# Gate rows made and stored during the first attention batch instead of after it, in a kernel of windowed attention and a four-expert mixture

## The chip, the cores and the metric

The kernel runs on one core of a Trainium2 chip. The metric is the device time of one execution, in microseconds (us). Three runs of the kernel before gave 365.98, 366.18 and 366.26 us; the median is 366.18 us. The profile is one further execution, recorded by the hardware profiler.

A core has a matrix engine (TensorE, here PE; its weight loads are shown apart as PEld), a vector engine (VectorE, DVE), an activation engine (ScalarE, ACT), GpSimd (POOL) and SyncE (SP). DMAs are issued from an engine's instruction stream, here from SP (q1 in the profile) and from POOL (q0), and all of them are carried out by the same 16 DMA engines. [...]

## The reference

Attention over 4 batches, 8 heads, 768 positions, 64 columns per head. A query sees the first 4 keys (sinks) and the last 128 keys. The result, 3072 tokens of 512 columns, goes through four experts, whose outputs are added with normalised weights:

```python
scores = scale * np.matmul(q, k.transpose(0, 1, 3, 2))
keep = is_sink | in_window
scores = np.where(keep, scores, -1000000000.0)
a = np.exp(scores - np.max(scores, axis=-1, keepdims=True))
a = a / (np.sum(a, axis=-1, keepdims=True) + 1e-09)
x = np.matmul(a, v)          # then heads side by side: (3072, 512)

p = domain_probs / (domain_probs.sum(-1, keepdims=True) + 1e-09)
for e in range(4):
    h = np.maximum(x @ w1[e], 0.0)         # w1[e]: 512 x 1024
    out += p[:, e:e + 1] * (h @ w2[e])     # w2[e]: 1024 x 512
```

The weight p of a token and an expert is called its gate.

## The kernel before

**Groups and units.** The tokens of a batch are three groups of 256: (b, 0), (b, 1), (b, 2). A unit is one group with one expert. The first layer of a unit makes H, the second layer adds it to the output.

**Two ways to apply the gate.** In groups (0, 0) and (0, 1) the second layer runs token by token (L1396), and the gate is applied to its result on DVE (L1406, L1408) as a scalar of each token. These scalars (`scale_t`) are made in `gates()`, with PE transposes of the raw gates (L907) and DVE operations (L909 to L912). From group (0, 2) on, the gate is applied to H itself, in the operation that empties a PSUM bank after the first layer (L1081, L1177). There the tokens lie along the free dimension, so each gate row of 256 tokens has to stand in all 128 partitions: a tile `gates` of 128 x 256 floats per unit.

**Where the gate tiles come from.** `gates_by_row()` works in `scratch`, where the raw gates of 24 blocks of 128 tokens lie since the start of the kernel: a sum over the experts, an addition, a reciprocal and a multiplication on DVE (L433 to L436), then two stores from SP to a DRAM tile `gate_rows` (L440). `load_gates()` asks for tiles in the order in which units will be opened (L456, SP), each a DMA that reads one row of 256 floats into 128 partitions. There are five buffers (NGATE): the first five tiles are asked for at once, a sixth when the unit that used the first is finished. `scratch` shares its buffer with the weight forms of expert 2 (`vf`), which come later.

**First and second layer.** A first layer is done plainly, in four tiles of eight matmuls of 256 columns (L1057, result `hps`), or with seven products in place of eight on sums of quarters (L1144, result `cps`), for which DVE makes forms of the weights (L376 to L382, L340 to L346) and differences of the tokens (L1113). The second layer of later groups is done likewise (L1318). Six PSUM banks are lent out in turn to all of these and to attention; two hold the second layer's sums.

**The order of the work.** The program is straight-line. Its order is found by a planner that runs while the program is built: it keeps a clock for each engine (`t["pe"]`, `t["dve"]`, ...), charges every operation an assumed time, and in a loop (from L1454) puts out the step that can start first, by priorities. `now` is PE's clock. Operations of ACT and DVE that follow a step are put on a list and put out by `flush` when the clock has come so far; some may go to either engine, whichever is free earlier. The planner does not know of the gate tiles' arrival: a unit is opened when its tokens, weights and banks are there. Each engine then works through its own instructions in the order written, waiting for semaphores.

**Order around the change.** Attention of batch 0 runs first, mixed with first and second layers of groups (0, 0) and (0, 1) once their tokens are ready. When its last step is out (`not att.more()`), a block of the loop runs once (`loaded`, L1460): gate rows, gate tiles, the list of loads of expert 3 and batch 1, and the list of DMA transposes of batch 1, which go on SP's queue (L245). From then on units of group (0, 2) may be opened (L1020). Weights and inputs are loaded by POOL, with a cast (L233, L298, L311, L321).

Of the kernel before, what the change touches and what calls it, by code (L numbers as in the profile page):

```python
# [16 lines left out]
def kernel(  # L17
# [63 lines left out]
    OPEN = 2.2  # L81
    SOON = 21000
    NEARLY = 2
    W2AT = 2
    ROWS1 = 1500
    ONACT = 1
# [30 lines left out]
    def dve(cols, *deps, rate=0.96, fixed=157):  # L117
        at = max([t["dve"], *deps])
        t["dve"] = at + fixed - 85 + cols / rate
        return at + fixed + 35 + cols / rate  # L120
# [232 lines left out]
    def spare_rows(e):  # L353

        spared[e] = [sb.tile([P, 2, H, D], BF16, name="qkn", tag="qkn", bufs=NQB) for _ in range(3)]
        spared_at[e] = qkn_free[2]
        del qkn_free[0:3]
# [28 lines left out]
    used, formed = set(), {}  # L386
    left = [NEARLY] * E

# [43 lines left out]
    def gates_by_row():  # L432
        nc.vector.reduce_sum(out=ds, in_=dp, axis=AX.X)  # L433
        nc.vector.tensor_scalar_add(out=ds, in0=ds, scalar1=1e-9)
        nc.vector.reciprocal(out=ds, in_=ds)
        nc.vector.tensor_mul(  # L436
            pn, dp.rearrange("n p e -> n e p"), ds[:, None, :].to_broadcast([NT, E, P]),
        )
        for i in range(2):
            nc.sync.dma_start(out=gate_rows[:, :, i, :], in_=pn[i:NT:2])  # L440
        dve(1800, 0.0)

    gate_sb = {}

    def load_gates():

        while len(gate_sb) < len(mix.order) and (
            len(gate_sb) < NGATE or mix.order[len(gate_sb) - NGATE] in mix.finished
        ):
            b, g, e = mix.order[len(gate_sb)]  # L450
            load_gate(b * NG + g, e)

    def load_gate(pair, e):

        x = mo.tile([P, 2, P], FP32, name="gates", tag="gates", bufs=NGATE)
        nc.sync.dma_start(  # L456
            out=x.rearrange("p t n -> p (t n)"), in_=gate_rows[pair, e].rearrange("t n -> (t n)").partition_broadcast(P),
        )
        gate_sb[pair, e] = x
        sp(takes=300)  # L460
# [362 lines left out]
    class Attention:  # L823


        def __init__(self, b):
            self.b = b
            self.flips = [("transposes", b, g, hp) for g in range(NG) for hp in range(NHP)] if not b else []
            self.todo, self.scored, self.valued = [], [], []
            for g in range(NG):  # L830
                if g == (1 if b == 0 else 0):
                    self.todo.append(("keys", b, 0, 0))
                self.todo += [("scores", b, hp, g) for hp in range(NHP)]
                if g and (b < ONE or g == 1):
                    self.todo.insert(2 - NHP if b == 0 else -NHP, ("sinks", b, g, 1 if b < ONE else 2))
            self.total = len(self.todo) + len(self.flips) + (1 if b else 2) * NG * NHP
            self.steps = 0
# [80 lines left out]
    QF = NFB // 2  # L918
    PAIRS = [(b, g) for b in range(B) for g in range(NG) if (b, g) >= (0, NEARLY)]
    CHAIN = ("P1", "P2", "P6", "P5", "P7", "P3", "P4")  # L920
# [3 lines left out]
    class Mixture:  # L924


        def __init__(self):
            self.early = {g: list(range(E)) for g in range(NEARLY)}
            self.open = []
# [159 lines left out]
        def tokens(self):  # L1089

            pairs = [x for x in [(0, g) for g in range(NEARLY)] + PAIRS if any(self.is_fast(*x, e) for e in FAST)]
            n = len(self.T)
# [128 lines left out]
        def chore(self):  # L1221
# [25 lines left out]
            if any(x[:2] < (b, g) and x[2] == "P5" for x in self.products) or any(x[:2] < (b, g) for x in self.last):  # L1247
                return False
            if (b, g) == PAIRS[0] and (len(self.stored) < 2 * NEARLY or self.stored[-1] > t["pe"] + 500):
                return False  # L1250
# [177 lines left out]
    mix = Mixture()  # L1428
    att = Attention(0)
    work = [sum(NFB * NDB * G * (1 if (b, g) < START[e] else 7 / 8) + NFB * NDB * G * (1 if (b, g) < PAIRS[0] else 7 / 8) for g in range(NG) for e in range(E)) for b in range(B)]  # L1430
    ahead, upto, loaded, wide = 0, 0.0, 0, 0
    loads, turns = [(load_nat, 0, tb) for tb in (4, 5)] + [(load_v, 0, (4, 5))], []
    for e in (1, 2):
        loads += [(load_w1, e), (load_w2, e)]
# [7 lines left out]
    def load_ready(x):  # L1442
        if x[0] is load_nat:
            return qkn_free[0]
        if x[0] is load_v and x[1]:
            return max(values_at.get((x[1] - 1, min(NG - 1, (tb + 1) // 2)), 1e12) for tb in x[2])
        return 0.0

    def free_ring(x):
        if ahead < 1 or turns and x[1] <= turns[0][0]:  # L1450
            return True
        return t["hw"] < t["pe"] and not (turns and (turns[0][0], 0) in turned_at)

    while mix.more() or att.more():  # L1454
        now = t["pe"]

        if not att.more() and ahead == B - 1 and not wide:
            wide = 1
            mix.widened()
        if not att.more() and not loaded:  # L1460
            loaded = 1
            gates_by_row()
            load_gates()
            turns += [(1, tb) for tb in range(NQB)]
            loads.append((load_w1, 3))
            for tb in range(NQB):
                if tb == W2AT:
                    loads.append((load_w2, 3))
                loads.append((load_nat, 1, tb))
                if tb % 2:  # L1470
                    loads += [(load_v, 1, (tb - 1,)), (load_v, 1, (tb,))]
        x = next((x for x in loads if load_ready(x) < now + 1500), None)
        if x and t["pool"] < now + 1500 and free_ring(x):
            loads.remove(x)
            x[0](*x[1:])
        if turns and (ahead < 2 or not mix.second) and landed.get(("qk", *turns[0]), 1e12) < now and (turns[0][0] <= ahead or turns[0][0] == ahead + 1 and not att.todo):
            x = turns.pop(0)
            turn_nat(*x)
            b = x[0]
            if b in (1, B - 1) and x[1] == NQB - 1:  # L1480
                spare_rows("w2" if b == 1 else "w1")
            if 0 < b < B - 1 and x[1] == NQB - 1:
                nc.gpsimd.tensor_copy(out=held, in_=qkT[b][:, 1, NHP - 1, S - 2:S])
                pool(2, turned_at[x])
                nat_loads(b + 1, range(NQB))
                turns += [(b + 1, tb) for tb in range(NQB)]
        flush(now)
        mix.tokens()
        mix.chore()
        if ahead or now > SOON:  # L1490
            next_form()
        if ahead + 1 < B and not att.more() and (ahead == 0 or (ahead + 1, 0) in turned_at) and (ahead == 0 or mix.done >= sum(work[:ahead]) * LEAD[ahead - 1]):
            ahead += 1
            att = Attention(ahead)
            upto = mix.done
        share = (sum(work[:ahead]) - upto) * SHARE_OF[max(ahead - 1, 0)]
        due = ahead == 0 or att.steps * share <= (mix.done - upto) * att.total
        opts = []
        if att.more():
            opts = [(max(r, now), (DUE if due else 3) - 0.1 * (step == "two"), "att", step) for r, step in att.options()]  # L1500
        s2, p = mix.second_ready(), mix.product_ready()
        behind = max(t["dve"] - now, 0.0) + 500 * sum(x[2] == "dve" and x[0] < now + 300 for x in pend)
        opts.append((max(p, now), HIGH_PRODUCT if behind > BEHIND or mix.live >= FULL else LOW_PRODUCT, "product", None))
        opts += [(max(f, now), p, "first", x) for f, p, x in mix.firsts()]
        opts.append((max(s2, now), 1 if mix.since >= 1 else LOW_SECOND, "second", None))
        soonest = min(o[0] for o in opts)
        if soonest > now + 40 and flush(soonest, True):
            continue
        if soonest < 20000 and soonest > now + 220:
            idle_products(acc[1], 1, G)  # L1510
            continue
        if soonest > 1e11:
            if mix.stored and mix.stored[-1] > now:
                t["pe"] += 200
            elif loads:
                x = loads.pop(0)
                x[0](*x[1:])
            else:
                turn_nat(*turns.pop(0))
            continue  # L1520
        r, _, kind, step = min(opts, key=lambda o: (o[0] > now + 40, o[0] if o[0] > now + 40 else 0, o[1]))
        assert r < 1e11
        if kind == "att":
            att.emit(step)
        elif kind == "first":
            mix.emit_first(step, r)
        elif kind == "product":
            mix.emit_product()
        else:
            mix.emit_second()  # L1530
# [36 lines left out]
```

## Time and profile before

| | |
|---|---|
| median of three runs | 366.18 us (365.98 to 366.26) |
| the profiled execution | 366.61 us |
| its span, first to last instruction | 364.9 us |
| mean granted clock of PE | 0.995 |
| busy: PE, PEld, DVE, ACT, POOL | 352.8, 302.6, 303.9, 162.7, 71.5 us |
| DMA moved | 37.79 MB, mean 104 GB/s |

The span is cut by the profile's views into waits (who stood still until whom), a chain (followed back from the last instruction to what released each step), and stretches with the busy time of each engine. The granted clock is the share of full speed at which PE was let run. Idle time of an engine that does not bound a stretch costs nothing.

### The profile page before, as it was taken

The page shows a single profiled execution, that of the slowest core. Times are in us where ns is not written, and L with a number is a line of the kernel's source. Part 1 is how long each engine was busy: PE and PEld are TensorE (multiplying, and loading weights), DVE is VectorE, ACT ScalarE, POOL GpSimd, SP SyncE. Part 2 cuts the span into 40 slices and gives each one's busy share as a digit, 9 for nine tenths or more (in the row PEclk, how much of TensorE's full clock was granted, in tenths as well). Part 3 has the DMA queues.
Part 4 walks back from the last instruction along what each step waited for, and adds up shares of the span by engine and source line. Part 5 has one row for each costly group of instructions (what it writes and reads, how often), then busy time and mean ns, then how long its engine had stood idle before and what let it go on. Part 6 is the DMA issues. An engine that isn't in the chain of part 4 may idle for free.

```text
span 364.9 us, 10705 instructions
## 1 busy us (share of the span) xinstructions
PE 352.8 (97%) x4476; PEld 302.6 (83%) x4484; DVE 303.9 (83%) x690; ACT 162.7 (45%) x415; POOL 71.5 (20%) x92
## 2 busy tenths in 40 slices
PE   7899995999999999999999999999999999999995
PEld 3585763866689898898998999899899999999984
DVE  6875965968799989889769999989879889899840
ACT  5864610626786264556454344444435333313110
POOL 8936113440434406001052000000000000000000
PEclk9999998999999999999999999999999999999999
DMA  9999999999999999318199923011211031110011
GB/s 166 168 181 195 210 210 200 181 135 153 143 117 162 180 162 122 61 43 104 31 137 167 136 72 59 25 55 41 59 42 48 25 81 59 31 43 18 3 59 58
DMA packets 117869, 37.79 MB, mean 104 GB/s; under 512 B 100676, under 2 KB 113316, under 8 KB 117820
## 3 DMA queue, kind: packets, MB, share of 16 engines
q0 software_dynamic: 77520, 17.31, 53.5%
q1 hardware_dynamic: 39244, 19.28, 26.8%
q8 instruction: 35, 0.57, 0.6%
q10 hardware_dynamic: 1056, 0.52, 0.5%
q14 instruction: 14, 0.11, 0.1%
HBM read 40.98 MB, written 6.34 MB: 130 GB/s over the span
## 4 chain that ended last, share of the span: by engine, by line
PE 87%; DMA 5%; DVE 4%; POOL 2%; ACT 1%; issue 1%; SPq 0%; DVEq 0%; ACTq 0%
PE acc L1318 34%; PE cps L1144 32%; PE hps L1057 9%; PE acc L1396 5%; PE sps L683 3%; PE od L749 2%; DMA w<-in_moe_w_dram 2%; DMA gates<-gate_rows 2%; DMA gate_rows<-scratch 1%; POOL qkn L233 1%; PE od L742 1%; POOL vx L298 1%; DVE aT L717 0%; DVE onat L779 0%; ACT aT L708 0%
## 5 line engine op out<-in xcount | busy, mean ns | idle before, releaser
L1144 PEld LDWEIGHTS <-w 128*128 128x128 bf16 x1184 | 72.6, 98 | 3.0 <-issue 1.6
L1318 PEld LDWEIGHTS <-H 128*128 128x128 bf16 x700 | 65.0, 98 | 8.0 <-issue 1.5
L1177 DVE SCALAR_TENSOR_TENSOR H<-cps,gates 128x512 bf16<-128x512 f32 x90 | 60.7, 684 | 0.1
L708 ACT ACTIVATE aT<-sps 128x512 bf16<-128x512 f32 (+1 forms) x96 | 46.9, 571 | 24.7 <-PE sps L683 24.7
L1318 PE MATMUL acc<-w,H 128*128 128x256 bf16 x420 | 55.4, 273 | 0.0
L1057 PE MATMUL hps<-xT,w 128*128 128x256 bf16 x352 | 44.9, 278 | 3.9 <-DVE H L1081 3.8
L1144 PEld LDWEIGHTS <-vf 128*128 128x128 bf16 x744 | 45.6, 98 | 1.2 <-issue 0.5
L1144 PE MATMUL cps<-T,w 128*128 128x128 bf16 x592 | 45.0, 219 | 0.6 <-DVE cps L1197 0.6
L1144 PE MATMUL cps<-xT,w 128*128 128x128 bf16 x592 | 43.7, 219 | 0.0
L788 ACT ACTIVATE onat<-od,R 128x64 bf16<-128x64 f32 x144 | 33.2, 323 | 23.0 <-DVE R L776 22.9
L1057 PEld LDWEIGHTS <-w 128*128 128x128 bf16 x352 | 34.0, 100 | 10.7 <-issue 4.9
L1190 ACT COPY cps<-cps 128x512 f32<-128x512 f32 x37 | 21.4, 578 | 47.6 <-PE cps L1144 27.5
L1144 PE MATMUL cps<-T,vf 128*128 128x128 bf16 x496 | 36.4, 219 | 0.0
L1368 ACT COPY osb<-acc 128x256 f32<-128x256 f32 x36 | 13.6, 377 | 50.5 <-PE acc L1318 50.5
L298 POOL DMA_DIRECT2D vx<-in_v_dram x24 | 21.4, 896 | 62.6 <-PE od L749 52.7
L1318 PEld LDWEIGHTS <-S 128*128 128x128 bf16 x320 | 30.4, 98 | 3.4 <-issue 0.2
L1197 DVE TENSOR_TENSOR cps<-H,cps 128x512 f32<-128x512 f32 x32 | 22.2, 693 | 9.7 <-PE cps L1144 8.4
L1396 PE MATMUL acc<-w,H 128*128 128x512 bf16 x120 | 29.3, 379 | 0.6 <-issue 0.3
L1318 PE MATMUL acc<-wf,H 128*128 128x256 bf16 x208 | 29.3, 273 | 0.0
L702 DVE TENSOR_TENSOR aT<-aT,mask 128x1024 bf16<-128x1024 bf16 (+1 forms) x36 | 22.8, 643 | 3.5 <-ACT aT L708 3.2
L1212 DVE TENSOR_TENSOR H<-H,cps 128x512 f32<-128x512 f32 x32 | 21.9, 684 | 2.7 <-PE cps L1144 2.6
L1396 PEld LDWEIGHTS <-H 128*128 128x128 bf16 x128 | 12.1, 98 | 12.1 <-issue 0.2
(128 smaller groups left out, 548.1 us busy)
## 6 DMA issues: line engine op xcount, KB each, us to landing
w<-in_moe_w_dram POOLq DMA_DIRECT2D x7, 1024.0 KB, 18.5
out_dram<-osb SPq DMA_DIRECT2D x21, 256.0 KB
gates<-gate_rows SPq DMA_DIRECT2D x40, 128.0 KB
vx<-in_v_dram POOLq DMA_DIRECT2D x24, 128.0 KB, 6.3
qkn<-in_q_dram POOLq DMA_DIRECT2D x22, 128.0 KB, 8.6
qkn<-in_k_dram POOLq DMA_DIRECT2D x22, 128.0 KB, 9.6
w<-in_moe_w_dram POOLq DMA_DIRECT2D x2, 512.0 KB, 9.0
kraw<-in_k_dram ACTq DMA_DIRECT2D x2, 256.0 KB
```

The lines of the kernel that those rows point to most:

```text
L298: nc.gpsimd.dma_start(out=vx[tb][:, :, 0:D], in_=v[b, :, tb * P:(tb + 1) * P, :].rearrange("h p d -> p h d"),)
L702: nc.vector.tensor_mul(a, a, m[:, None, :].to_broadcast([P, 2, w]))
L708: nc.scalar.activation(out=a[:, ph], in_=sps[ph][:, 0:w], func=AF.Exp, scale=scale)
L788: nc.scalar.mul(o[:, qi, hp, ph * D:(ph + 1) * D], od[:, qi, ph, 0:D], R[:, qi, ph])
L1057: nc.tensor.matmul(h[:, i].rearrange("p (q n) -> p q n", q=2), lhsT=w1_sb[e][:, db, fb * P:(fb + 1) * P], rhs=xT[b, g][:, :, db], start=(i ...
L1144: nc.tensor.matmul(y[:, f], lhsT=A[:, d, f * P:(f + 1) * P], rhs=T[:, d], start=(m in ("P1", "P5") and f == 0 and d == 0), stop=(d == 1), ...
L1177: nc.vector.scalar_tensor_tensor(out=dst, in0=src, scalar=0.0, in1=gate, op0=ALU.max, op1=ALU.mult)
L1190: nc.scalar.copy(out=tiles["Y"], in_=y)
L1197: nc.vector.tensor_add(tiles["V"], c5, tiles["X"])
L1212: nc.vector.tensor_add(c5, c5, y)
L1318: nc.tensor.matmul(x, lhsT=self.operand(b, g, e, m)[:, f], rhs=forms[e][m][:, f], start=(k == 0 and f == 0 and m in (("P1", "P5", "P2") if ...
L1396: nc.tensor.matmul(op, lhsT=H[:, fb // QF, fb % QF, s], rhs=w2_sb[e][:, fb, :], start=(fb == 0), stop=(fb == NFB - 1),)
```

## The change

The making and storing of the gate rows and the request for the first gate tiles leave the block that runs after batch 0's attention. They get a condition of their own: the first time that PE's planned clock is past 24000 (ns) at the head of the loop. The block keeps its loads and transposes. The planner's charge for the four DVE operations goes from 1800 to 2800 columns.

```diff
+    ROWED = 24000
...
         for i in range(2):
             nc.sync.dma_start(out=gate_rows[:, :, i, :], in_=pn[i:NT:2])
-        dve(1800, 0.0)
+        dve(2800, 0.0)
...
+        if not rowed and now > ROWED:
+            rowed = 1
+            gates_by_row()
+            load_gates()
         if not att.more() and not loaded:
             loaded = 1
-            gates_by_row()
-            load_gates()
             turns += [(1, tb) for tb in range(NQB)]
             loads.append((load_w1, 3))
```

The four DVE operations, the two stores and the loads of the tiles are the same instructions as before; their places in the streams of DVE and SP differ, and whatever the planner orders otherwise because its clocks differ.

More of the change, by code (lines that the diff above doesn't have):

```diff
@@ L1430 @@
     work = [sum(NFB * NDB * G * (1 if (b, g) < START[e] else 7 / 8) + NFB * NDB * G * (1 if (b, g) < PAIRS[0] else 7 / 8) for g in range(NG) for e in range(E)) for b in range(B)]
-    ahead, upto, loaded, wide = 0, 0.0, 0, 0
+    ahead, upto, loaded, wide, rowed = 0, 0.0, 0, 0, 0
     loads, turns = [(load_nat, 0, tb) for tb in (4, 5)] + [(load_v, 0, (4, 5))], []
```

## The prediction

> **What bounds the kernel now.** I read the page's first and fourth parts, then the waits of the matmul engine (PE), the chain of waits, and the stretches between 46 and 75 us.
>
> ```profile
> span 364.9 us, 10705 instructions
> PE 352.8 (97%) x4476; PEld 302.6 (83%) x4484; DVE 303.9 (83%) x690; ACT 162.7 (45%) x415; POOL 71.5 (20%) x92
> ```
>
> PE is the bound: 352.8 of 364.9 us. What can be won is the 12 us in which it stands still, and time at a lower clock. The waits of PE (total, times, longest):
>
> ```profile
> PE hps L1057 <- DVE H L1081: 3.8, 1, 3.8
> PE cps L1144 <- DVE cps L1197: 0.6, 1, 0.6
> ```
>
> The 3.8 us are one wait: the first-layer tiles of group (0,2) for expert 0 find no free PSUM bank, because VectorE (DVE) has not multiplied the earlier tile by its gate. The chain of waits, in order of time (start, us, what), says why DVE is late:
>
> ```profile
> 43.89 0.95 DVE scratch L435
> 44.86 1.07 DVE scratch L436
> 46.92 5.42 DMA gate_rows<-scratch
> 52.39 6.15 DMA gates<-gate_rows
> 59.38 3.52 PE hps L1057 x16
> ```
>
> The gate rows are made at 43 to 46 us, stored, and read back as tiles: two DMAs in series, 11.6 us, landing at 58.54. The stretches around it (columns: span, PE, PEld, DVE, ACT, POOL busy, PE clock, DMA share, GB/s):
>
> ```profile
> 46.00:55.60 9.60, 9.55 (x64) 6.18 (x64) 5.84 (x12) 1.79 (x3) 1.75 (x2) 1.00 1.24 207
> 55.60:59.40 3.80, 0.04 (x2) 0.01 (x1) 0.76 (x2) 0.00 (x0) 0.17 (x1) 0.97 1.85 209
> 59.40:62.80 3.40, 3.40 (x18) 2.29 (x18) 3.37 (x6) 0.00 (x0) 1.75 (x3) 0.53 1.95 198
> 66.00:67.00 1.00, 0.41 (x9) 0.29 (x7) 1.00 (x3) 0.42 (x1) 1.00 (x2) 1.00 1.29 210
> 75.00:361.00 286.00, 285.72 (x3797) 256.02 (x3798) 248.26 (x549) 125.70 (x342) 35.65 (x42) 1.00 0.64 82
> ```
>
> PE is empty from 55.6 to 59.4, then runs 3.40 us at clock 0.53, and has one more hole at 66 while DVE works off its backlog. From 75 to 361 us it misses only 0.28 us. So all that this change can give lies between 55 and 67 us.
>
> **The change part by part.** *Where the rows go.* The new condition is looked at once per planned step, in the planner's own clock. That clock charges a first-layer tile 8 x 256 / 2.4 + 8 x 2.5 = 873 ns, the step of the tiles in the row at 23.05 below (40 matmuls, five tiles; the last four are group (0,1)). Following its arithmetic, 24000 is first passed ahead of the third tile of that group, which is at 23.05 + 3 x 0.87 = 25.7 us in the trace. At that point the last DVE work put out is the fourth token difference. DVE in order of time (start, us, operation, idle before):
>
> ```profile
> 24.19 0.28 DVE L1113 TENSOR_TENSOR T<-xT,T 128x256 bf16<-128x256 bf16 x1
> 24.39 0.68 DVE L376 TENSOR_TENSOR vf<-w 128x1024 bf16<-128x1024 bf16 x1
> 28.20 0.26 DVE L909 TENSOR_REDUCE rs<-acc 128x24 f32<-128x96 f32 x1 [2.40 <-PE acc L907]
> 31.77 0.75 DVE L1406 TENSOR_SCALAR osb<-acc,scale_t 128x512 f32<-128x512 f32 x1 [0.97 <-PE acc L1396]
> 34.38 0.75 DVE L1406 TENSOR_SCALAR osb<-acc,scale_t 128x512 f32<-128x512 f32 x1 [1.54 <-PE acc L1396]
> 42.94 0.67 DVE L433 TENSOR_REDUCE scratch<-scratch 24x128 f32<-24x512 f32 x1
> 58.64 0.69 DVE L1081 SCALAR_TENSOR_TENSOR H<-hps,gates 128x512 bf16<-128x512 f32 x1 [6.66 <-DMA gates<-gate_rows]
> ```
>
> *The four DVE operations.* They run from 42.94 to 44.86 + 1.07 = 45.93, so 2.99 us, of which nothing is saved. Moved, they run from 24.47 to 27.46. The weight forms of L376 and L378 step back behind them (by the planner's clock behind the scale operations of L909 too). Idle stretches of 2.40, 0.97 and 1.54 us, 4.9 in sum, take the 3 us before anything of PE waits; were they not there, PE would lose at most the 2.99 us. I take 0. The other end: DVE, busy 5.84 us of the time from 46 us to the start of its long idle (58.64 - 6.66 = 51.98), is 2.99 us freer there; PE, busy 9.55 of 9.60 us, can't turn that into time.
>
> *Larger planner cost (1800 to 2800).* No instruction; it moves planned times only, see the plan below.
>
> *SP's queue.* SyncE, in order of time:
>
> ```profile
> 2.42 5.69 SPq L473 DMA_DIRECT2D vsf<-in_v_dram  x8
> 45.96 1.73 SPq L440 DMA_DIRECT2D gate_rows<-scratch  x2
> 52.39 12.93 SPq L456 DMA_DIRECT2D gates<-gate_rows  x6
> 65.51 5.93 SPq L245 DMA_TRANSPOSE qkT<-qkn  x2
> ```
>
> SP is empty from 8.1 to 46 us, so the two stores and five loads, and the wait of the loads for the stores, hold up nothing. Row stores: issued at 27.5, landed 52.39 - 45.96 = 6.4 us later, 33.9. First tile 6.15 us on, 40.0; all five some 9 us after the first issue, 43. The first is wanted when DVE gets to it, at 51.98. So 9 to 12 us to spare and the 6.66 us idle of DVE goes. The sixth load waits for a gate buffer, and batch 1's transposes are behind it; both come earlier by the same shift, and their first reader is PE's row at 83.59 below, far off. POOL's queue gets nothing and is passed by nothing.
>
> *What goes.* PE's wait, 3.76 us. The half clock behind it: 3.40 x (1 - 0.53) = 1.60 us. The hole at 66, where DVE at 100% was catching up: 0.59 us. Sum 5.95 us.
>
> *What it collides with.* Five tiles of 128 x 256 floats are 0.66 MB, the rows 0.05. They now move while weights are being read, and two of those are wanted soon. PE's rows, POOL's issues, and the time to landing of the two loads (w1 and w2 of expert 1, last column):
>
> ```profile
> 23.05 4.53 PE L1057 MATMUL hps<-xT,w 128*128 128x256 bf16 x40
> 38.62 1.04 PE L1057 MATMUL hps<-xT,w 128*128 128x256 bf16 x8
> 44.19 1.89 PE L1396 MATMUL acc<-w,H 128*128 128x512 bf16 x7
> 83.59 0.50 PE L683 MATMUL sps<-qkT 64*128 64x256 bf16 x8
> 21.90 0.75 POOL L311 DMA_DIRECT2D w<-in_moe_w_dram  x1 [1.35 <-DMA w<-in_moe_w_dram]
> 27.66 0.88 POOL L321 DMA_DIRECT2D w<-in_moe_w_dram  x1 [5.00 <-DMA w<-in_moe_w_dram]
> w<-in_moe_w_dram POOLq DMA_DIRECT2D x1, 1024.0 KB, 15.1
> w<-in_moe_w_dram POOLq DMA_DIRECT2D x1, 1024.0 KB, 14.4
> ```
>
> w1 lands at 37.0 and is read at 38.62: 1.6 us to spare. w2 lands at 42.06 and is read at 44.19: 2.1 us. What the gate tiles took from the weights is in the DMA queues (packets, MB, share of 16 engines), first from 52.4 to 56.2 us, then from 56.2 to 61.2:
>
> ```profile
> q0 software_dynamic: 1432, 0.72, 140.5%
> q1 hardware_dynamic: 8, 0.01, 0.8%
> ...
> q0 software_dynamic: 3265, 0.44, 131.3%
> q1 hardware_dynamic: 712, 0.65, 48.6%
> ```
>
> The weights fell from 0.72 / 3.8 = 0.19 to 0.44 / 5.0 = 0.09 MB per us for five us: 0.5 MB pushed back, at 207 GB/s 2.5 us. And the tiles' packets began only 3.8 us after the first issue. Carried over: they move from about 37.7 to 42.7, w1 (37.0) is gone by then, w2 comes at most 2.5 us late, 44.6 against 44.19. Cost 0.4 us. One end is 0: the tiles come after w2's own packets. The other is a start without the lag of 3.8 us, for stores and tiles both: the stores land near 30, the tiles run from 30 to 35, w1 comes at 37.0 + 2.5 = 39.5 against 38.62, PE waits 0.9 us there and no more at w2. I take the lag, since the q1 row shows it.
>
> [...]
>
> *The plan behind it.* From 42 us on the planner sees DVE earlier by its old charge (about 1.9 us), so operations that either engine may take, and steps that come free a little sooner, can change place. Matmul work is the same either way. The trace before has no row for another order. It can win at most the 0.28 us that PE still misses after 75; it can lose a wait like those of the trace, 0.6 or 3.8 us. I take 0.6, the nearest of its kind (PE on DVE behind a backlog).
>
> *Sum.* -5.95 + 0.4 + 0.6 = -4.95 us. The profiled execution took 366.61 us in all (span 364.9 and 1.7 around it), 0.43 above the median of 366.18. So 361.7 for that execution, 361.2 against the median.
>
> **The rivals.**
>
> *Tiles without the lag.* The 0.9 us above in place of 0.4: 361.7.
>
> *Weights late.* The tiles drag on, at the rate of the row from 56.2 to 61.2 but for ten us in place of five: 10 x (0.19 - 0.09) / 0.207 = 4.9 us, so w2 at 47.0 and a wait of 2.8 us. 366.18 - 5.95 + 2.8 + 0.6 = 363.6, with 363 to 364.5 around it. For: only 1.6 and 2.1 us to spare. Against: the bytes are few, 0.71 MB is 3.4 us at 207 GB/s in all.
>
> *DVE takes its place: slower.* DVE is full when batch 1 begins its own experts:
>
> ```profile
> 60.00:70.00 10.00, 9.96 (x17) 0.87 1.71 193
> 100.00:110.00 10.00, 9.96 (x23) 1.00 1.36 119
> 110.00:120.00 10.00, 10.00 (x26) 1.00 1.61 163
> ```
>
> (Columns: span, DVE busy, PE clock, DMA share, GB/s.) PE arrives there about 5 us sooner. If DVE did not, or if the new order put another 2 to 3 us of its work in these 20 us, PE would wait for it one for one, and a wait near 4 us also costs 1.6 us of clock, as at 59. It decides when the waits pass 5.95 us, say one of 4.0 with its 1.6 of clock and one of 2.0: 7.6, so 366.2 + 7.6 - 5.95 = 367.9 us. For: no slack in these rows. Against: DVE gains the 6.66 us of idle at 52 that PE's lead comes from, so both arrive earlier together.
>
> *The change does not do it: same.* If the rows are put behind something late, or SP held, the tiles still land near 51 to 58 and the wait remains: 366.2. SP's empty queue and the free DVE from 24 to 35 speak against it.
>
> *Small loss by the new order.* A second wait of 2 to 3 us somewhere after 75: 363 to 364.5.
>
> **How the numbers follow.** Forecast (gain 3.2 to 6.3): 0.65, its own range 359.9 to 363.0; 0.12 of that are tiles without the lag. Weights late, 363 to 364.5: 0.13. Small loss by order, the same span: 0.08. Same: 0.04. DVE takes its place: 0.10. A difference under 0.2% (0.7 us) is about what a measurement of this kernel can't tell from none. Faster 0.86, same 0.04, slower 0.10. Lower bound: 366.18 - 5.95 - 0.28 with no collision, 359.95; a little under, 359.7. Upper: beyond 365.2 lie the last two cases, 0.14.
>
> **What would show it.** Right: the four operations near 24.5 to 27.5 on DVE, the stores right behind on SP, the gate tiles landed before 45, no wait of PE on L1081, clock 1.00 from 55 to 65, DVE without the 6.66 us idle. The collision: a wait of PE on the weight DMA near 44 of 0.4 us (or near 39 of 0.9). Wrong: such a wait over 2 us, DMA landings of w1 and w2 over 3 us later, a new idle of PE over 1 us between 75 and 361, or the gates' DMA still ending DVE's wait.

## The result and the profile after

The changed kernel takes 361.65 us (median of six runs, 361.21 to 363.26) against 366.08 us of the kernel before beside it. The ratio is 0.9884, with a 95% interval of 0.9867 to 0.9900: 1.2% faster. Two later comparisons, each on a chip of its own, gave 0.9888 (0.9858 to 0.9917) and 0.9869 (0.9851 to 0.9886).

The profiled execution of the changed kernel took 363.26 us, the slowest of its six; the second profile of it, below, shows in which waits. One line was added above most of the code, so line numbers are mostly one higher than before. The first lines of the page:

```profile
span 361.5 us, 10704 instructions
PE 351.5 (97%) x4476; PEld 302.4 (84%) x4484; DVE 303.8 (84%) x691; ACT 162.4 (45%) x414; POOL 71.7 (20%) x92
```

The span is 3.4 us shorter and PE is busy 1.3 us less: it did the same 4476 matmuls, but none at half clock (1.00 in every stretch up to 357.6 us). The stretches that had carried the loss (span, PE, PEld, DVE, ACT, POOL busy, PE clock, DMA share, GB/s):

```profile
46.00:55.60 9.60, 9.28 (x61) 6.13 (x63) 5.98 (x10) 1.79 (x3) 1.75 (x2) 1.00 1.19 209
55.60:59.40 3.80, 3.80 (x31) 2.66 (x29) 3.64 (x7) 0.00 (x0) 0.87 (x1) 1.00 1.77 180
59.40:62.80 3.40, 3.40 (x62) 3.28 (x60) 3.40 (x6) 2.04 (x4) 1.34 (x2) 1.00 2.26 163
66.00:67.00 1.00, 1.00 (x22) 1.00 (x20) 1.00 (x4) 1.00 (x3) 0.65 (x1) 1.00 1.26 205
75.00:357.60 282.60, 281.52 (x3762) 253.25 (x3762) 244.09 (x542) 124.14 (x339) 35.40 (x42) 1.00 0.67 84
```

PE is full from 55.6 to 62.8 and at 66, at clock 1.00. But from 75 us to the end of the matmuls it now misses 1.08 us where it missed 0.28. The waits of PE that are new, in the same view as before (total, times, longest):

```profile
PE acc L1397 <- DMA w<-in_moe_w_dram: 1.3, 1, 1.3
PE hps L1058 <- DMA w<-in_moe_w_dram: 0.9, 1, 0.9
PE sinks L645 <- DVE qkn L345: 0.8, 1, 0.8
```

The wait for the gate is gone. In its place stand a wait for the second-layer weights of expert 1, one at the very start for the first expert's weights, and one at the sink scores of batch 1. Where PE stands at these three waits, and at its first tile with seven products in place of eight (59.23), in the changed kernel:

```profile
19.73 0.50 PE L1058 MATMUL hps<-xT,w 128*128 128x256 bf16 x3 [0.90 <-DMA w<-in_moe_w_dram]
...
46.21 1.89 PE L1397 MATMUL acc<-w,H 128*128 128x512 bf16 x7 [1.32 <-DMA w<-in_moe_w_dram]
...
59.23 0.61 PE L1145 MATMUL cps<-xT,w 128*128 128x128 bf16 x8
...
89.45 0.29 PE L645 MATMUL sinks<-qkT,ksd 128*32 128x256 bf16 x4 [0.85 <-DVE qkn L345]
```

and the kernel before at the first of them, at that tile, and at the sink scores:

```profile
19.11 1.05 PE L1057 MATMUL hps<-xT,w 128*128 128x256 bf16 x8 [0.15 <-DMA w<-in_moe_w_dram]
...
62.74 0.28 PE L1144 MATMUL cps<-xT,w 128*128 128x128 bf16 x2
...
92.80 0.29 PE L644 MATMUL sinks<-qkT,ksd 128*32 128x256 bf16 x4
```

So this execution was 0.62 us behind at 19 us, before anything of the change, and 2.02 us behind at the second layer (46.21 against 44.19). At the first tile with seven products it was 3.51 us ahead (59.23 against 62.74). Between these two places it gained 2.02 + 3.51 = 5.53 us, close to the wait and the half clock of the prediction (3.76 + 1.60 = 5.36). The last stretch of matmuls starts 3.36 us sooner (338.53 against 341.89).

The rows and tiles went where the prediction put them. DVE and SP in order of time:

```profile
24.94 0.67 DVE L434 TENSOR_REDUCE scratch<-scratch 24x128 f32<-24x512 f32 x1
...
26.87 1.07 DVE L437 TENSOR_TENSOR scratch<-scratch 24x512 f32<-24x512 f32 x1
28.75 0.26 DVE L910 TENSOR_REDUCE rs<-acc 128x24 f32<-128x96 f32 x1 [0.82 <-PE acc L908]
```

```profile
27.96 1.72 SPq L441 DMA_DIRECT2D gate_rows<-scratch  x2
34.66 26.13 SPq L457 DMA_DIRECT2D gates<-gate_rows  x6
...
77.77 5.61 SPq L246 DMA_TRANSPOSE qkT<-qkn  x2
83.48 0.55 SPq L1415 DMA_DIRECT2D out_dram<-osb  x1
```

The second pair of transposes in the kernel before:

```profile
77.68 4.89 SPq L245 DMA_TRANSPOSE qkT<-qkn  x2
```

The four operations take 3.00 us and end at 27.94; the stores are issued at 27.96; the first tile load 6.7 us later.

Instruction by instruction, the streams of PE, POOL and SP are in the same order in both kernels. DVE's differs by the rows' place and a few neighbours, and one copy went from ACT to DVE. The planner ordered hardly anything else otherwise.

### The profile page after: what moved, and what is told of

Same layout as the page of the kernel before. It is cut to its first block, busy times and chain, and to the rows that moved or that the text cites. A ratio compares the mean times of both kernels' runs of the same rounds, so it can differ in the third digit from the quotient of the medians.

```text
span 361.5 us, 10704 instructions
## 1 busy us (share of the span) xinstructions
PE 351.5 (97%) x4476; PEld 302.4 (84%) x4484; DVE 303.8 (84%) x691; ACT 162.4 (45%) x414; POOL 71.7 (20%) x92
## 4 chain that ended last, share of the span: by engine, by line
PE 86%; DMA 11%; DVE 1%; issue 1%; ACT 1%; POOL 0%; ACTq 0%; POOLq 0%; DVEq 0%
PE acc L1319 34%; PE cps L1145 32%; DMA w<-in_moe_w_dram 9%; PE hps L1058 7%; PE acc L1397 6%; PE sps L684 3%; PE od L750 2%; DMA kraw<-in_k_dram 2%; PE od L743 1%; PE sinks L645 0%; ACT aT L709 0%; POOL w L312 0%; DVE qkn L345 0%; DVE qkn L343 0%; ACT qkn L270 0%
## 5 line engine op out<-in xcount | busy, mean ns | idle before, releaser
L1058 PE MATMUL hps<-xT,w 128*128 128x256 bf16 x352 | 43.3, 273 | 0.9 <-DMA w<-in_moe_w_dram 0.9
L1198 DVE TENSOR_TENSOR cps<-H,cps 128x512 f32<-128x512 f32 x32 | 22.1, 691 | 9.8 <-PE cps L1145 8.4
## 6 DMA issues: line engine op xcount, KB each, us to landing
w<-in_moe_w_dram POOLq DMA_DIRECT2D x7, 1024.0 KB, 18.3
```

The costliest lines, as they stand in the source:

```text
L1058: nc.tensor.matmul(h[:, i].rearrange("p (q n) -> p q n", q=2), lhsT=w1_sb[e][:, db, fb * P:(fb + 1) * P], rhs=xT[b, g][:, :, db], start=(i ...
L1198: nc.vector.tensor_add(tiles["V"], c5, tiles["X"])
```

## The experiments

Two theories at the start. The first: the gain is the removed wait with its half clock, and what is missing from it is DMA time, the tiles' packets pushing back loads that PE then waits for. The rival: part of gain and loss comes from the other order on DVE and ACT.

### Early rows in the old order

```diff
-        dve(2800, 0.0)                 # in gates_by_row
...
             loaded = 1
+            dve(1800, 0.0)
```

> Rows and tiles early as in the changed kernel, but the planner's charge stays where and what it was (1800, when attention is over), so that ACT's stream and the rest of DVE's are those of the kernel before. If the gain is the gate wait alone, this one gains as much as the changed kernel: 361.7 us within 0.6, with the wait for the second-layer weights near 46 us of about 1.3. If part of the gain or loss comes from the other order on DVE and ACT, it lies more than 0.7 us off.

In the traces the order of every stream is that of the kernel before, apart from the four operations. 361.72 us, ratio 0.9866 (0.9835 to 0.9896): all of the gain, without the new order. Its profiled execution took 361.55 us, and after 20 us PE waits for one thing of note:

```profile
PE sinks L644 <- DMA qkT<-qkn: 1.0, 1, 1.0
```

The weights' wait that I expected there is absent. The sink scores' wait stands, and here the view names the DMA, batch 1's transposes, and not DVE. It is the same wait in the changed kernel: there the last of these transposes landed at 89.31 us by the trace, and the sink scores started at 89.45.

### Late rows in the new order

```diff
         if not rowed and now > ROWED:
             rowed = 1
-            gates_by_row()             # its own charge is taken out
-            load_gates()
+            dve(2800, 0.0)
...
             loaded = 1
+            gates_by_row()
+            load_gates()
```

> The streams of ACT and the rest of DVE as in the changed kernel (charge of 2800 at 24000), but the four operations, stores and tile loads back after attention. If the order alone does nothing: 366.1 us within 0.7, wait of PE on L1081's successor of about 3.8 and the half clock behind it. If the order is worth something of its own: below 365.

In the traces the order is that of the changed kernel, apart from the four operations. 365.94 us, ratio 0.9982 (0.9962 to 1.0002). The order alone is worth nothing that can be told from zero; the wait is back, 2.98 us and then 0.67, and so is the half clock:

```profile
58.74 1.19 PE L1057 MATMUL hps<-xT,w 128*128 128x256 bf16 x8 [2.98 <-DVE H L1081]
60.59 1.86 PE L1057 MATMUL hps<-xT,w 128*128 128x256 bf16 x8 [0.67 <-DVE H L1081]
```

```profile
60.00:61.00 1.00, 0.41 (x3) 0.27 (x3) 1.00 (x2) 0.00 (x0) 0.69 (x1) 0.50 1.77 221
61.00:62.00 1.00, 1.00 (x6) 0.71 (x5) 0.97 (x3) 0.00 (x0) 0.55 (x1) 0.50 2.43 155
```

The rival falls: place of the rows, not order, makes the difference.

### Early rows, tiles held back

```diff
-            load_gates()               # behind gates_by_row() in the early block
...
             loaded = 1
+            load_gates()
...
         x = mo.tile([P, 2, P], FP32, name="gates", tag="gates", bufs=NGATE)
+        if not gate_sb:
+            nc.vector.memset(x[:, 0, 0:2], 0.0)
```

> Rows made and stored early, but the first gate tile's load has to follow a small write of DVE to that tile, put out when attention is over (near 42 us); the other four are behind it on SP. If the wait for the second-layer weights near 46 us (1.3 us) comes from the tiles' packets, it goes, the weights land near 42.5 in place of 46.2, and the time falls by 0.6 to 1.3 us below the changed kernel: 360.4 to 361.0. If that wait has another cause, it stays and the time is 361.7. If the tiles now come too late for L1081, DVE waits for them near 53 and the time rises above 362.

361.59 us, ratio 0.9851 (0.9829 to 0.9873). No wait for the second-layer weights is left, and none for the tiles; the sink scores' wait of 0.8 us stays. In time it is not the 360.4 to 361.0 expected but level with the early rows in the old order on the same chip (361.72), which had no such wait either. So the tiles cost a wait in some executions, and a gain in time from holding them is not shown. How long the weights take from issue to landing (last column), in the kernel before, with the tiles held back, and in the changed kernel:

```profile
w<-in_moe_w_dram POOLq DMA_DIRECT2D x1, 1024.0 KB, 14.4
```

```profile
w<-in_moe_w_dram POOLq DMA_DIRECT2D x1, 1024.0 KB, 14.8
```

```profile
w<-in_moe_w_dram POOLq DMA_DIRECT2D x1, 1024.0 KB, 18.3
```

In two more profiles of the changed kernel it was 17.3 and 17.0 us, with the early rows in the old order 17.3. The tiles hold this load up by 2.2 to 3.9 us (17.0 against 14.8, 18.3 against 14.4). Whether PE feels it depends also on when POOL issued it: at 26.24 us with the early rows in the old order (landed 43.54, read at 44.17, no wait), at 27.91 us in the changed kernel's first profile (landed 46.21).

### Twice the tiles

```diff
+        if len(gate_sb) < NGATE:
+            nc.sync.dma_start(
+                out=twice[len(gate_sb)], in_=gate_rows[pair, e].rearrange("t n -> (t n)").partition_broadcast(P),
+            )
```

> The changed kernel with five more loads beside the first five, the same 128 rows of 256 floats each, into a DRAM tile that nobody reads: 0.66 MB more in the same stretch. [...]

364.11 us, ratio 0.9920 (0.9891 to 0.9949): 2.4 us lost against the early rows in the old order on the same chip. I had expected the loss at the second-layer weights of expert 1; it lies elsewhere for the most part:

```profile
PE sinks L651 <- DMA qkT<-qkn: 1.9, 1, 1.9
PE sps L690 <- DMA qkT<-qkn: 1.8, 1, 1.8
...
PE acc L1403 <- DMA w<-in_moe_w_dram: 0.4, 1, 0.4
```

The 0.66 MB more hardly reached the weights of expert 1 (issue to landing 18.3 us, against 17.0 to 18.3 without them). They pushed back what came behind: the transposes of blocks 2 and 3 were issued at 79.38 us, against 75.61 with the early rows in the old order. There PE waits 3.7 us. The extra loads are the price, and here most of it is paid at these transposes; whether their bytes or their number of packets count, this run does not separate. In this execution the clock stayed at 1.00.

### The changed kernel, profiled again

> The changed kernel itself, profiled a second time. If its first profile (363.26 us, weights' wait of 1.3 us) was an execution whose first loads came late, this one shows about 361.6 us, the second-layer weights landing 1 to 2.5 us sooner, a weights' wait near 0, and still 0.8 to 1.0 us of wait for batch 1's transposes near 88. If the weights' wait is always there: 1.3 again.

362.28 us, ratio 0.9888, profiled execution 362.25 us:

```profile
PE sinks L645 <- DMA qkT<-qkn: 1.0, 1, 1.0
PE acc L1397 <- DMA w<-in_moe_w_dram: 0.3, 1, 0.3
```

A third profile, beside the last experiment, gave 1.1 and 0.8 us. So the weights' wait was 1.32, 0.33 and 0.83 us, the transposes' wait 0.85, 1.00 and 1.13. The first profile was the slowest by its waits: 0.90 us for the first expert's weights (0.3 in the second) and 1.32 for the second-layer weights (0.33). That the lateness of the first loads went on to the second-layer weights, as I expected, is not shown. POOL issued that load at nearly the same time in all three, at 27.91, 27.73 and 27.78 us; it then took 18.3, 17.3 and 17.0 us. The third profile had no wait for the first expert's weights and still 0.83 for the second-layer ones.

### One load of 1 MB behind batch 1's rows

```diff
         nat[b, tb] = both
+        if (b, tb) == (1, 3):          # and no longer in load_w2 for expert 3
+            nc.gpsimd.dma_start(out=w2_sb[3], in_=moe_w2[3].rearrange("(fb p) d -> p fb d", p=P))
```

> The changed kernel with one load moved in POOL's queue: the second-layer weights of expert 3 (1 MB) behind the rows of batch 1's blocks 2 and 3 in place of ahead of them; all other streams as they are. If PE's wait near 88 is for the transposes of blocks 2 and 3, whose rows come late, these land some 4 us sooner, the wait goes, and the time is 0.8 to 1.0 us under the changed kernel: 360.7. If that wait is DVE's (as the view of waits names it): unchanged, 361.6. If expert 3's weights now come too late for their first use near 80: above 362.

> Both moves: tiles held until attention is over, and expert 3's second-layer weights behind blocks 2 and 3. If the two waits are separate: no wait of PE over 0.5 us after 20 us, 360.5 to 360.8. If removing one only uncovers another: 361.4 or more.

368.61 us, ratio 1.0052 (1.0031 to 1.0073), and 367.68 us, ratio 1.0032 (1.0012 to 1.0052): slower than the kernel before, the third outcome. The load was issued at 62.7 us and took 22.1 us, landing at 84.8. PE's waits in the first of the two (3.6 and 0.8 us in the second):

```profile
PE acc L1400 <- DMA w<-in_moe_w_dram: 4.1, 1, 4.1
PE sps L687 <- DMA qkT<-qkn: 1.6, 1, 1.6
```

I had taken the loads to change places. But POOL stood still before several of its loads until an earlier one had landed (3.93 us before the first of batch 1's rows, 4.14 before the second), so the moved load was issued at 62.7 us against 55.36 in the second profile of the changed kernel. The runs do not answer the question that they were made for.

### Rows a little sooner than the end of attention

```diff
             rowed = 1
+            dve(2800, 0.0)             # the charge alone
+        if rowed == 1 and now > 40500:
+            rowed = 2
             gates_by_row()
             load_gates()
```

> The order of the changed kernel with the rows made at 40500 of the planner's clock, about 1.7 us of DVE's work sooner than in the run with the rows after attention (wait of PE 3.0 in one piece and half clock behind it). The tiles land some 1.7 us sooner and the wait shrinks to about 1.3. If the half clock needs a wait of about 3 us, it is gone too, clock 1.00 throughout: 365.9 - 1.7 - 1.6 = 362.6. If any wait over 1 us costs the clock: 364.2.

364.14 us, ratio 0.9942 (0.9920 to 0.9964). That this is the number of the second outcome is chance, for the mechanism was neither of the two. The rows now stand in front of two operations of attention's last step, and PE waits for them, in a profiled execution of 365.68 us, the slowest of its ten:

```profile
46.68 0.28 PE L807 MATMUL tx<-ident,onat 128*128 128x128 bf16 x2 [2.01 <-DVE onat L779]
```

The gate's wait shrank to 0.34 us because PE itself was late, by this wait and by 1.98 us for the first expert's weights. Two readings can be taken from it. The four operations do cost PE 2.0 of their 3.0 us where DVE has no idle time to take them. And in this execution no clock was lost after a wait of 2.01 us:

```profile
46.00:48.00 2.00, 1.32 (x11) 1.11 (x13) 1.93 (x6) 0.12 (x1) 0.00 (x0) 1.00 1.23 207
48.00:50.00 2.00, 1.95 (x13) 1.12 (x12) 1.86 (x7) 0.47 (x1) 0.87 (x1) 1.00 1.23 209
```

### Two small loads behind batch 1's rows

```diff
+            if b != 1 or tb > 1:       # load_v issues all but batch 1's blocks 0 and 1
+                fetch_v(b, tb)
...
         nat[b, tb] = both
+        if (b, tb) == (1, 3):
+            fetch_v(1, 0)
+            fetch_v(1, 1)
```

> The changed kernel with two small loads moved in POOL's queue: the values of batch 1's blocks 0 and 1 (128 KB each) behind the rows of blocks 2 and 3, so that these and the 1 MB of expert 3 in front of them start 1 to 2 us sooner; all other streams as they are. If PE's wait of 1.0 us near 88 is for the transposes of blocks 2 and 3 and these follow their rows, the wait shrinks by the same 1 us or goes: about 1 us under the changed kernel, ratio to the kernel before near 0.986. If the transposes are late for another reason (their own packets among the loads): the wait stays at 0.8 to 1.0, ratio 0.988 to 0.989. If the values come too late for their first use near 83: slower.

361.85 us, ratio 0.9869 (0.9845 to 0.9893). The transposes' wait stays:

```profile
PE sinks L652 <- DMA qkT<-qkn: 1.2, 1, 1.2
```

They were issued 1.6 us sooner (74.99 against 76.59 in the second profile of the changed kernel), but they landed only 0.7 us sooner (87.62 against 88.30), and PE reached the sink scores 0.87 us sooner too, in part because it did not wait for the weights (0.33 us). So the wait stays, as in the second outcome, though the ratio is nearer to the first. The tiles-held run and the early rows in the old order had these transposes issued at 75.6 us without this move, so what the move itself did is not shown.

> The same with the tiles held until attention is over. If both waits (weights near 45, transposes near 88) are for DMAs that come sooner now, neither is left over 0.3 us, and the ratio to the kernel before is 0.984 to 0.986. If the transposes' wait stays: 0.987.

360.92 us, ratio 0.9859 (0.9839 to 0.9880). With the tiles held back as well, neither wait is left: the longest of PE after 20 us is 0.3 us. The last transposes land at 86.08 us here, against 87.33 with the tiles held and the values unmoved.

### Side by side

> The changed kernel once more, on the same chip as the next run. 361.3 to 362.3 us, a wait of 0.8 to 1.2 for the transposes near 88 and 0 to 1.3 for the weights near 45, depending on when the first loads land.

> Tiles held until attention is over and values of blocks 0 and 1 behind the rows of blocks 2 and 3, as before: both waits under 0.3 us. If these waits are what the change still costs: 0.8 to 1.3 us under the changed kernel on the same chip. If they only move: within 0.4 of it.

On one chip, the changed kernel took 361.55 us (ratio 0.9869, 0.9851 to 0.9886), the kernel with both moves 361.13 us (0.9855, 0.9838 to 0.9871). Its profile has neither of the two waits, only 1.3 us for the first expert's weights, a wait that other runs here had too (0.90 in the first profile of the changed kernel, 1.98 with the rows at 40500). The medians differ by 0.42 us, and the intervals overlap: the waits are gone, a gain in time over the changed kernel is not shown.

## Why the prediction was right, point by point

The forecast was 361.2 us, -4.95 us; measured were 361.65 us and -4.43.

- **The rows' place and cover.** Right. 3.00 us of DVE work at 24.94, behind the token differences and before the scale operations; no wait of PE from it. The bound for the case without cover, at most 2.99 us, has a measured value now: 2.01 us.
- **What goes, -5.95 us.** Right, all three parts: no wait for the gate, clock 1.00 from 55.6 to 62.8, no hole at 66. The first two gave 5.53 us in the profiles, against 5.36 forecast.
- **The lag of the tiles.** Right. First tile issued at 34.66 against 33.9 predicted; hardware-queue packets from 34 to 38 us and from 38 to 46 us, in the changed kernel:

```profile
q1 hardware_dynamic: 8, 0.00, 0.3%
...
q1 hardware_dynamic: 719, 0.66, 31.1%
```

  The tiles took nearly 8 us and not the five assumed. The lag from the first issue to the bulk of the packets is more than 3 us here (34.66 to 38) as before (3.8 us from 52.4); where it comes from is not shown.
- **The collision, +0.4 us.** Right mechanism, size too small. The weights took 2.2 to 3.9 us longer, predicted 2.5; PE waited 0.33, 0.83 and 1.32 us in three profiles of the changed kernel, once more than either end of the forecast (0 and 0.9), and not at all where POOL issued the load at 26.24.
- **The plan behind it, +0.6 us.** Wrong. Nothing of PE's order changed, and the order that did change cost nothing measurable (0.9982, up to 1.0002, which is 0.1 us). That the sum came out near is luck: something else, not in the sum, took this term's place.
- **What took its place, in the step on SP's queue.** There I wrote that the transposes' first reader, PE's row at 83.59, was "far off". That is the pair of blocks 0 and 1. I also wrote that the transposes come earlier by the same shift as the tiles. Blocks 2 and 3 do not, since they are transposed from rows that POOL loads: issue started at 77.68 before, and at 77.77, 76.59 and 76.33 in the three profiles after. Before, the last of them landed at 88.74 by the trace, and their reader, the sink scores, stood at 92.80: 4.06 us to spare. After, they landed at 89.31, 88.30 and 88.25, while PE came to the sink scores 4.20, 5.36 and 5.55 us sooner; it waits 0.85, 1.00 and 1.13 us. The spare time was less than the lead of about 5 us that the prediction itself gives PE. I checked one reader of the queue and not the next.
- **DVE takes its place.** Did not happen: in the three profiles of the changed kernel PE waits for nothing over 0.3 us after the sink scores near 88.

Profile against profile, the changed kernel's first execution should differ by -5.95 + 0.62 (late at 19 us) + 1.32 + 0.85 = -3.2 us; it did by 363.26 - 366.61 = -3.35. For the second profile: -5.95 + 0.33 + 1.00 = -4.6, against 362.28 - 366.29 = -4.0 by the medians beside it. For the early rows in the old order: -5.95 + 1.01 = -4.9, against 361.72 - 366.72 = -5.0. The terms close to 0.6 us or better, though the last two sums set the waits of one execution against medians of several.

## What to carry to other kernels

Where a wait ends in a chain of two DMAs, look for a place earlier at which the engines that feed the chain are idle. Here such a place was worth the wait plus the clock lost behind it: 5.53 us in the profiles, against 3.76 + 1.60 us forecast. The lead so won is spent on whatever is tied to something that did not move: here a lead of 4.20 to 5.55 us met 4.06 us to spare at batch 1's transposes, and PE waited 0.85 to 1.13 us. So list every later reader of each DMA that keeps its time, not the first alone, and compare its spare time with the lead. Look also at the loads around a transfer that is brought forward: here the second-layer weights of expert 1 took 2.2 to 3.9 us longer, about what the tiles' bytes give as an estimate (0.66 MB at the 207 GB/s of the kernel before from 46 us on are 3.2 us). The price can show later: with twice the tiles it was some 40 us later, at the transposes (waits of 1.9 and 1.8 us).

## What the runs showed of the hardware

The granted clock fell to 0.50 in or behind a gap of PE of 3.76 us in the kernel before, of 2.98 with the rows late, and of 4.14 and 3.61 in the two runs with 1 MB moved. It stayed at 1.00 around gaps of 1.98 and 2.01 us with the rows at 40500, and of 1.84 us with twice the tiles. The fall did not come at one distance from the start of the gap: 3.5 us after it in the kernel before and 3.7 with the rows late, but 1.0 and 1.2 us in the two runs with 1 MB moved.

The half clock lasted 3.41 us in the kernel before (59.15 to 62.56) and with the rows late (59.48 to 62.90), and 6.83 us in the two runs with 1 MB moved (81.68 to 88.51 and 80.50 to 87.33). In the trace of the kernel before, the stretches at one granted clock last 54.61, 3.413 and 303.79 us, which is 16, 1 and 89 times 3.413; in that of the changed kernel the first lasts 354.99 us, 104 times 3.413. The last stretch of each, which the record's end cuts, is shorter (0.58 and 3.11 us). Counted in such stretches, the last one ahead of the fall held 0.00 us of PE's work in the kernel before and 1.49 in both runs with 1 MB moved. With the rows late it held 0.74, and the clock fell when PE was already at work again, behind a gap of 2.98 us:

```profile
56.07:59.48 3.41, 0.74 (x7) 0.67 (x7) 1.49 (x3) 0.00 (x0) 0.88 (x1) 1.00 1.84 211
59.48:62.90 3.42, 2.75 (x18) 1.93 (x17) 3.39 (x6) 0.00 (x0) 2.32 (x3) 0.50 1.99 196
```

In the first run with 1 MB moved, the clock fell 1.0 us into the gap of 4.1 us (80.72 to 84.86); the gap of 1.6 us before it (77.65 to 79.23) ended in the same stretch:

```profile
78.27:81.68 3.41, 1.49 (x16) 1.01 (x16) 1.40 (x4) 1.66 (x5) 0.87 (x1) 1.00 1.85 89
```

With the rows at 40500, the gap of 2.01 us fell across two stretches, and the clock stayed at 1.00:

```profile
42.40:45.81 3.41, 2.27 (x26) 1.73 (x22) 3.31 (x6) 2.10 (x4) 0.88 (x1) 1.00 1.14 206
45.81:49.23 3.42, 2.49 (x17) 1.64 (x19) 3.25 (x11) 0.60 (x1) 0.58 (x1) 1.00 1.23 207
```

So in these traces the stretch ahead of a fall held from 0.00 to 1.49 us of PE's work. A bound cannot be read off: the two stretches above, with 2.27 and 2.49 us, kept the clock, but so did one with 1.43 us of work at the start of the same profile (18.51 to 21.92, with the gap of 1.98 us in it) and one with 1.57 in the run with twice the tiles (with the gap of 1.84 us in it). Executions of one kernel differ too: with the rows at 40500 the mean granted clock was 0.993 to 0.995 in five of ten, as low as in the kernel before with its one stretch at half clock (0.995), and 0.998 or more in the other five. What decides is not shown.

In the profile of the changed kernel the first tile load was issued from SP at 34.66 us, and its queue sent 8 packets up to 38 us and 97 in the microsecond after, while POOL's loads moved 0.82 MB in the four us from 34 to 38, 0.2 MB per us. What holds such loads up is not shown. PE's wait for the first expert's weights differed between executions, from none to 1.98 us; whether that makes a later wait appear is not shown either.
